# One load moved forward in SP's queue: the residual rows of channel block 2, in a layered convolution and attention kernel

## The chip, the cores and the metric

The kernel runs on one core of one Trainium2 chip. The metric is the device time of one execution in microseconds (us); lower is better. The engines are named as the profile names them: PE (matmuls; PEld are its weight loads), DVE (vector engine), ACT (scalar engine), POOL, and SP, which here only issues transfers to the DMA engines.

## What is computed

Two kinds of layer alternate on an array x of 2048 positions by 512 channels, each added to x after a layer norm:

```python
x = A_u
x = x + _A_ref(_layernorm(x), ...)   # long convolution by FFT over the 2048 positions, one filter per channel
x = x + _B_ref(_layernorm(x), ...)   # local attention: 32 heads of 16, window of 8 at stride 2
x = x + _A_ref(_layernorm(x), ...)
x = x + _B_ref(_layernorm(x), ...)
return x

# inside _A_ref
K = jnp.einsum("dn,dnl,dn->dl", Cc, P, dB).real          # the filters, from the state-space parameters
Yf = Uf * Kf                                             # spectra of u and of K, length 4096
y = irfft2(Yf)[..., :L]; return y + u * Dskip
```

## The kernel before

The work is four stages in a row: `prepare` with `kernel_and_first_conv`, a first `b_layer`, `a_layer`, and a second `b_layer`. The change lies in `kernel_and_first_conv`, which makes the filters K, their spectra, and the first convolution.

The 512 channels are four blocks of 128, dc = 0 to 3. The array X stays in SBUF as 128 partitions of 16 rows of 512 channels, in two halves of 256. For each block the function does this:

- `tables` and `contract` make the filter from products of tables (DVE, then PE in many small matmuls, lines 488 and 491), and `store` and `fetch` turn it by way of DRAM (lines 839 and 846).
- `spectrum` transforms the block of u, and likewise the block of K: a first set of matmuls (line 862), ACT's copy into Z (line 867), a transpose of Z either by DMA (`turn`, line 876) or by PE and ACT (lines 893 and 897), a second set of matmuls (lines 882 to 885), ACT's copy (line 889). `keep` (line 944) stores the spectrum of K in DRAM for the later `a_layer`.
- `residual` (line 928) loads the block's columns of the input once more into X, in place of the normed columns that `spectrum` has read. It must come after the block's first matmuls, and `final` needs it. It is 512 KB in 2,048 pieces of 256 bytes.
- `product` multiplies the two spectra (DVE, lines 952, 957 and 958), `inverse` transforms back (PE lines 972 to 976, copies into VT at line 979), and `final` (lines 996 and 999) adds the residual rows by a matmul with the identity and the result of the last transform, and is copied into X (line 1003).

The last half block of K (half of block 3) has a way of its own, `last(n)` for n = 0 and 1: `spread_rows` (line 1021), copy (1025), first matmuls (1035 and 1037), copy (1040), transpose by PE (1046), copy (1050), second matmuls (1056 and 1057), copy (1061).

What is issued in what order is written out by hand. Every piece of work is an operation of a plan, numbered in the order in which the code names it, and a list of numbers in `ORDERS` gives the order in which they are issued:

```python
order = [int(i) for i in ORDERS[Plan.turn].split()]
for i in order:
    fn, after, way = self.ops[i]
    fn()
```

Each engine takes its own operations in this order, and waits for what each of them needs. Two operations on different engines are ordered only by such a need. The operations that the text speaks of, by engine in their order before the change:

| engine | operations |
|---|---|
| SP | 669 load of the last filter block (line 846); 387 and 577 stores of K's spectra (line 944); 683 transpose of the last spectrum by DMA (line 876); 579 and 580 stores; **355 the reload of block 2** (line 928); 688, 689 and 578 stores |
| PE | 686 second matmuls of the spectrum that 683 turned; 705 first matmuls of `last(0)`; 646 and 656 inverse of block 2 (lines 972, 976); 715 `spread_rows` of `last(1)`; 708 transpose of `last(0)`; 636 inverse of block 2; 718 first matmuls of `last(1)`; 711 second of `last(0)`; 666 `final` of block 2 |
| DVE | 654 join (lines 957, 958) for 656; 633 product and 634 join for 636; 728 and 738 products of block 3 |
| ACT | 682 copy for the store 688; 706 copy of 705's result; 647 copy of 646's; 657 of 656's; 716 of 715's; 709 of 708's |

Op 633 writes into one of two buffers, the one that 646 has read; 728 and 738 wait in the same way for 656 and 636. The pool of accumulators in PSUM has three buffers.

Of the kernel before, what the change touches and what calls it, by code (L numbers as in the profile page):

```python
# [198 lines left out]
def load_params(nc, pp, prm):  # L199
# [33 lines left out]
    "375 431 461 433 533 463 492 494 536 548 526 495 499 498 585 496 539 497 540 500 549 550 553 555 551 556 554 610 "  # L233
    "611 612 613 616 552 586 546 388 449 587 439 617 534 544 572 557 529 618 619 545 614 441 620 622 567 530 451 443 "
    "535 575 562 669 588 589 592 593 598 453 576 560 472 387 561 473 604 469 570 470 670 672 571 671 599 605 673 674 "
    "676 606 675 623 690 691 577 677 692 693 608 679 565 694 624 609 702 680 566 681 682 607 626 627 703 683 579 643 "
    "653 644 696 697 580 698 699 700 654 686 705 355 687 646 706 656 715 647 657 716 708 633 634 709 636 728 738 637 "
    "718 688 711 689 720 666 712 721 722 663 724 578 668 729 739 664 725 727 714 731 748 741 750 732 743 758 759 757 "
    "744 761 762 777 771 768 778 772 774 769 775",
    "82 0 50 136 7 57 84 39 1 93 156 86 128 85 44 154 87 155 40 142 13 241 262 130 58 199 200 201 99 190 263 264 125 "  # L240
# [1791 lines left out]
```

## Time and profile before

| | |
|---|---|
| three runs | 470.94 us median, 469.26 to 471.42 |
| the profiled execution | 470.51 us, of which the span from the first to the last instruction is 468.7 |
| busy in the span | PE 393.3 us (84%), PEld 242.7 (52%), DVE 440.0 (94%), ACT 348.1 (74%), POOL 21.2 (5%) |
| mean granted clock of PE | 0.996 of full speed |
| instructions of PE | 5,229 matmuls and 5,248 weight loads |
| transfers of line 928 | 4, of 512 KB each, 4.9 to 5.8 us from issue to landing, median 5.3 |
| `kernel_and_first_conv` | its last copies into X (line 1003) end at 202 us |

Times inside an execution are counted from the start of the span. A line of a timeline gives the start, the duration, the engine, the source line, the operation, what it writes and reads, and how many were merged (x2). In brackets stands how long the engine was idle before it, and which event the profile holds responsible. A wait for several events is put down to the last of them; where the engine named was done long before, it was something else. "issue" means that nothing in the profile explains the wait. A line of the table by windows gives, for a stretch of time, the busy time of each engine with the number of instructions, the clock granted to PE, the mean busy share of the 16 DMA engines and the GB/s they moved.

### The profile page before, as it was taken

Reading aid. Unit: us, or ns where it says so; the run is one execution under the profiler, and the core shown is the slowest. Engines: PE = TensorE matmul, PEld = TensorE weight load, DVE = VectorE, ACT = ScalarE, POOL = GpSimd, SP = SyncE. Lnnn points to the kernel's source line nnn. Section 1 sums busy time; section 2 is a strip of 40 time slices with the busy share of each in tenths; the row PEclk is TensorE's granted clock in tenths of the full one; section 3 lists DMA queues with packets and bytes.
Section 4 is the critical chain, followed back from the end, with each engine's and each line's share of the span. In section 5 each row is a group of like instructions: output and inputs, shape, how many; then the busy total and the mean of one; then the engine's idle time right before and its main releaser. Section 6 shows DMA issues by size and latency. Waiting matters only on the chain. (4 is left out here: it accounts for less than half of the span.)

```text
span 468.7 us, 12362 instructions
## 1 busy us (share of the span) xinstructions
PE 393.3 (84%) x5229; PEld 242.7 (52%) x5248; DVE 440.0 (94%) x595; ACT 348.1 (74%) x543; POOL 21.2 (5%) x90
## 2 busy tenths in 40 slices
PE   2520876788899997899999979979999999998996
PEld 1310543545666666654476434556776445563453
DVE  6999999999999995879999999999996899999995
ACT  6999867896888886657797357999996667763452
POOL 1000000000000000500000000000000000100210
PEclk9999999999999998999999999999999999999999
DMA  8991163138597564840112230379957200213584
GB/s 233 189 304 71 14 150 91 21 73 162 140 178 148 126 140 134 138 69 1 62 47 78 57 67 2 69 247 183 170 100 111 58 18 18 79 46 78 61 155 123
DMA packets 111419, 49.36 MB, mean 105 GB/s; under 512 B 88811, under 2 KB 104572, under 8 KB 111108
## 3 DMA queue, kind: packets, MB, share of 16 engines
q1 hardware_dynamic: 109924, 47.70, 46.9%
q0 software_dynamic: 1152, 0.61, 1.1%
q8 instruction: 41, 0.67, 0.6%
q10 hardware_dynamic: 288, 0.26, 0.2%
q14 instruction: 14, 0.11, 0.1%
HBM read 15.88 MB, written 8.13 MB: 51 GB/s over the span
## 5 line engine op out<-in xcount | busy, mean ns | idle before, releaser
L1755 DVE TENSOR_TENSOR prod<-VX,L 128x512 bf16<-128x512 bf16 (+2 forms) x72 | 75.2, 1100 | 0.5
L1579 DVE TENSOR_TENSOR prod<-qT,kT 128x4096 bf16<-128x4096 bf16 (+1 forms) x40 | 72.3, 1859 | 1.6 <-ACT qT L1504 1.5
L1771 PE MATMUL po<-prod,sb_ident 128*128 128x512 bf16 x216 | 51.7, 379 | 2.5 <-DVE prod L1755 1.1
L1771 PEld LDWEIGHTS <-sb_ident 128*128 128x128 bf16 x224 | 21.7, 98 | 27.8 <-issue 2.5
L450 PE MATMUL ps_sum<-Ttab,sb_ident 128*128 128x512 bf16 x36 | 14.7, 407 | 22.1 <-DVE Ttab L411 20.6
L1534 PE MATMUL ps_v<-wv,U 128*128 128x256 bf16 x256 | 31.3, 272 | 1.0 <-ACT L L1718 0.3
L867 ACT CAST Z<-ps_s 128x1024 bf16<-128x1024 f32 (+1 forms) x32 | 29.3, 986 | 3.2 <-PE ps_s L862 2.6
L1855 PE MATMUL ps_o<-wo_t,oT 128*128 128x512 bf16 x122 | 31.4, 379 | 0.2
L1545 ACT ACTIVATE VX<-ps_v,rs 128x256 bf16<-128x256 f32 x64 | 26.6, 472 | 4.5 <-PE ps_v L1534 4.1
L1480 PE MATMUL ps_qk<-U,wqk 128*128 128x512 bf16 x128 | 29.7, 379 | 0.2 <-ACT qT L1485 0.2
L1534 PEld LDWEIGHTS <-U 128*128 128x128 bf16 x256 | 24.4, 98 | 8.9 <-issue 4.3
L1499 PE MATMUL ps_qk<-U,wqk 128*128 128x512 bf16 x128 | 29.0, 379 | 0.0
L475 DVE TENSOR_TENSOR Ttab<-Ttab,MPA 128x2048 bf16<-128x2048 bf16 (+2 forms) x20 | 28.3, 1428 | 0.1
L1789 ACT CAST ot<-po 128x1024 bf16<-128x1024 f32 x14 | 13.9, 1013 | 18.0 <-PE po L1771 18.0
L475 DVE TENSOR_TENSOR Y2tab<-Ttab,MPB 128x6144 bf16<-128x6144 bf16 (+1 forms) x13 | 27.2, 2117 | 0.0
L952 DVE TENSOR_TENSOR pa<-sp_u,sp_k 128x2048 bf16<-128x2048 bf16 x16 | 19.3, 1219 | 5.9 <-PE vp L976 4.3
L488 PE MATMUL psk<-Ttab 128*32 128x64 bf16 x1024 | 20.1, 197 | 4.3 <-DVE Ttab L475 3.1
L455 ACT CAST Ttab<-ps_sum 128x1024 bf16<-128x1024 f32 (+1 forms) x22 | 18.1, 869 | 7.0 <-PE ps_sum L451 6.9
L488 PEld LDWEIGHTS <-Ttab 128*32 128x32 bf16 x1024 | 18.0, 95 | 8.8 <-issue 7.4
L412 DVE TENSOR_TENSOR Ttab<-Ttab,MUB 128x256 bf16<-128x256 bf16 (+4 forms) x36 | 22.3, 619 | 0.0
L1590 PE MATMUL Lp<-prod,sb_bones 128*32 128x512 bf16 x256 | 19.7, 382 | 2.6 <-DVE prod L1579 2.4
L491 PE MATMUL psk<-Y2tab,Ttab 128*32 128x48 bf16 x1024 | 19.8, 190 | 1.8 <-DVE Y2tab L475 1.2
(255 smaller groups left out, 1018.0 us busy)
## 6 DMA issues: line engine op xcount, KB each, us to landing
kt_scratch<-sp_k SPq DMA_DIRECT2D x16, 256.0 KB, 4.1
Kt<-kt_scratch SPq DMA_DIRECT2D x16, 256.0 KB, 5.4
X<-in_A_u_dram SPq DMA_DIRECT2D x8, 256.0 KB, 5.4
X<-in_A_u_dram SPq DMA_DIRECT2D x4, 512.0 KB, 5.3
out_dram<-X SPq DMA_DIRECT2D x16, 128.0 KB, 2.3
k_scratch<-KTq SPq DMA_DIRECT2D x7, 256.0 KB, 2.3
KT<-k_scratch SPq DMA_DIRECT2D x7, 256.0 KB, 3.4
VX<-VX SPq DMA_DIRECT2D x4, 448.0 KB, 3.8
```

The costliest lines, as they stand in the source:

```text
L412: nc.vector.tensor_tensor(self.spare(hc, False)[:, x0:x1, :, :, 0:m, :].rearrange("n x h c e t -> n (x h c) e t"), src, mult(1), ALU.mult)
L475: nc.vector.tensor_tensor(d, src.to_broadcast([128, c, n, 2 * EYB]), mm, ALU.mult)
L488: nc.tensor.matmul(o.rearrange("e (s i) -> e s i", s=2), xs, T[:, 1:3, h, m // 2, :, t], start=(m == 0), stop=False, skip_group_check=True)
L867: nc.scalar.copy(box["Z", kind, dc][:, 0:n // 8, :, jq * 32:(jq + 1) * 32].rearrange("p g r k -> p r g k"), box.pop(("s1", kind, dc, jq))[ ...
L1480: nc.tensor.matmul(ps[:], wqk[:, ct, f0:f0 + 128], XT[:, ct // 2, 4 * s:4 * s + 4, ct % 2, :], start=(ct == 0), stop=(ct == 3))
L1499: nc.tensor.matmul(box[name][:, k * 512:k * 512 + 512], wqk[:, ct, f0:f0 + 128], XT[:, ct // 2, 4 * s:4 * s + 4, ct % 2, :], start=(ct == ...
L1534: nc.tensor.matmul(ps[:, jj].rearrange("p t h d -> p (t h d)"), XT[:, ct // 2, j + jj, ct % 2, :], wv[:, ct, fp * 256:(fp + 1) * 256], sta ...
L1545: nc.scalar.activation(out, ps, ACT.Identity, scale=r)
L1579: nc.vector.tensor_tensor(pr[:], windows(q, 0, 2), windows(kT[fp][:, a:a + n2, col(w):col(w) + 1024], -DIL * 128, 2), ALU.mult)
L1755: nc.vector.tensor_tensor(p2[:].rearrange("p w j t d h -> p w (j t) d h"), windows(v, -DIL * 256, taps), l.to_broadcast([128, taps, nj * 2 ...
L1771: nc.tensor.matmul(po[:, c:c + 512], ident[:], p2[:, t, k + j:k + j + 2].rearrange("p j t d h -> p (j t d h)"), start=first, stop=stop)
L1855: nc.tensor.matmul(ps, oT[:, ft // 2, o:o + 128], wo_t[:, ft, :], start=(ft == 0 and not res), stop=(ft == 3))
```

## The change

Op 355, the reload of block 2's residual rows, stands 32 places further ahead in the second list of `ORDERS`: right behind op 577 and ahead of op 677, instead of behind op 705. The order of all other operations stays the same. On SP's queue it passes three operations: 683, 579 and 580. No other function or size is changed.

```diff
-    "676 606 675 623 690 691 577 677 692 693 608 679 565 694 624 609 702 680 566 681 682 607 626 627 703 683 579 643 "
-    "653 644 696 697 580 698 699 700 654 686 705 355 687 646 706 656 715 647 657 716 708 633 634 709 636 728 738 637 "
+    "676 606 675 623 690 691 577 355 677 692 693 608 679 565 694 624 609 702 680 566 681 682 607 626 627 703 683 579 "
+    "643 653 644 696 697 580 698 699 700 654 686 705 687 646 706 656 715 647 657 716 708 633 634 709 636 728 738 637 "
```

## The prediction

> **What bounds the kernel now.** I read the page first. DVE is busy for 94% of the span, PE for 84%. The chain that ended last is followed back only to 421.99 us, far behind the change, so it says nothing here; the stage itself has to be read. The moved reload is the fourth transfer of line 928, and the timeline of SP has it at 174.92:
>
> ```profile
> 164.22 0.57 SPq L846 DMA_DIRECT2D KT<-k_scratch  x1
> 164.85 1.30 SPq L944 DMA_DIRECT2D kt_scratch<-sp_k  x2
> 171.22 2.55 SPq L876 DMA_TRANSPOSE zt<-Z  x1
> 173.83 1.05 SPq L944 DMA_DIRECT2D kt_scratch<-sp_k  x2
> 174.92 0.56 SPq L928 DMA_DIRECT2D X<-in_A_u_dram  x1
> 175.63 4.05 SPq L944 DMA_DIRECT2D kt_scratch<-sp_k  x3
> ```
>
> SP is done with op 577 at 166.15 and then waits until 171.22, when ACT's last copy of the spectrum (line 867) ends. Who reads the reload? Op 666, PE's first matmul of line 996 for block 2, at 188.90. The transfers of line 928 land in 5.3 us at the median, this one by about 180.2: nobody waits for its data, and by that reading alone the move is worth nothing. So I read the stretches around it, with the table by windows (columns: stretch, length, busy time of PE, weight loads, DVE, ACT, POOL, granted clock, DMA share, GB/s):
>
> ```profile
> 168.50:171.80 3.30, 2.76 (x165) 2.48 (x162) 3.30 (x6) 3.03 (x6) 0.00 (x0) 1.00 0.03 9
> 174.50:177.00 2.50, 2.34 (x139) 1.94 (x137) 2.50 (x4) 2.41 (x3) 0.00 (x0) 1.00 0.80 223
> 177.00:179.70 2.70, 2.66 (x45) 1.92 (x44) 2.14 (x5) 2.44 (x4) 0.00 (x0) 1.00 1.05 251
> 179.70:182.30 2.60, 0.00 (x0) 0.00 (x0) 1.99 (x3) 1.09 (x2) 0.00 (x0) 1.00 0.67 234
> 182.30:184.30 2.00, 1.99 (x16) 1.70 (x16) 0.44 (x1) 0.51 (x1) 0.00 (x0) 0.62 0.07 20
> 184.30:186.30 2.00, 2.00 (x21) 1.99 (x20) 0.79 (x1) 1.09 (x2) 0.00 (x0) 0.53 0.00 0
> ```
>
> Until 179 DVE is full (the last table products). Then follows a chain of PE, ACT and DVE steps up to the last copies into X at 202, and in it PE stands still for 2.6 us and then runs at about half clock for 3.4 us, while the DMA engines are full from 174.5 to 181.5 and were empty from 168.5 to 171.8.
>
> Why does PE stand still? The timelines of PE and DVE:
>
> ```profile
> 178.73 0.41 DVE L958 TENSOR_TENSOR pa<-pa 128x512 bf16<-128x512 bf16 x1
> 182.31 0.27 PE L972 MATMUL vp<-sb_IC,pa 128*128 128x256 bf16 x1 [2.64 <-DVE pa L958]
> 111.39 0.39 PE L450 MATMUL ps_sum<-Ttab,sb_ident 128*128 128x512 bf16 x1 [0.88 <-issue]
> 141.12 0.38 PE L884 MATMUL xp<-zt,sb_C 128*128 128x512 bf16 x1 [1.02 <-issue]
> ```
>
> The named releaser ended at 179.14, before PE stopped at 179.66; PE had even loaded op 656's first weights at 179.39. So it was something else. Two other stops (0.88 and 1.02) are inside a group of matmuls that need nothing new, and are put down to "issue". Counting PE's weight loads and matmuls in order of time, the three stops come after instructions 3,262, 4,542 and 6,334: the differences, 1,280 and 1,792, are 5 and 7 times 256. And the DMA part of the page has a queue that carries instructions:
>
> ```profile
> q8 instruction: 41, 0.67, 0.6%
> ```
>
> 41 packets of 16 KB for PE's 10,477 instructions are 256 instructions each. Narrowing the DMA view to single packets gives their times: 108.34 to 110.08, 138.78 to 139.70, 179.93 to 180.97. PE resumes 1.31, 1.42 and 1.34 us after each of them ends. PE stands still because its next block of instructions is not there. The 24th block was due to be asked for when PE entered the block before, at 175.9; its packet starts 4.0 us later. The two blocks ahead of it started 0.2 us before and 1.0 us after that point (166.53, 171.83). What lies in those 4.0 us is the reload: 2,048 pieces of 256 bytes, which run from 176.5 to 179.8. The block's packet comes just behind them.
>
> **The change, part by part.** Nothing is added or removed. SP issues op 355 straight after op 577, past three operations of its own queue: the transpose 683 and the stores 579 and 580. No other engine's order changes, POOL's queue has nothing here.
>
> *The issue itself.* One issue of 0.56 us goes from 174.92 to about 166.2. It lies in SP's wait up to 171.22 (5.1 us), so it costs nothing; without that cover it would delay the transpose by 0.56. The matmuls of block 2's forward transform, which it must follow, ended before 149 (the later reload of block 3 is issued then), so it adds no wait. Behind it on SP stand 683, 579, 580; 683 feeds PE's op 686 at 176.74.
>
> *The transfer.* In front of it are the load of line 846 and two stores, whose packets end at 168.5. The reload's pieces took about 3 us, so here they run from 168 to 171 through the empty stretch and land by about 171.5 to 172. The transpose's packets begin at 172.2. Nothing collides; from below nothing is gained, from above the transpose waits out the whole 3 us: it landed 4.0 us after its issue, at 175.2, 1.5 before its reader, so at most 1.5 us are lost on PE. I take nothing, the nearer row being the DMA share of 0.03.
>
> *What leaves 176.5 to 179.8.* Ahead of the 24th block remain the stores 579 and 580 (packets over at about 176.7) and 688, which waits for ACT until 175.60 and stays at 175.63. With the start of the two blocks before (0.2 before to 1.0 after the point), a length of 1.04 to 1.57 and 1.3 to 1.4 to arrive, it is there between 178.0 and 179.9; PE needs it at 179.5. If it waits for all of 688 too (8 packets of 84 ns on each engine, 0.7), 180.6. The stop shrinks from 2.64 to between 0 and 1.1; I take 0.2.
>
> *The clock.* It fell at 182.78 for 3.41 us, after the 2.64 us stop and not after those of 0.88 and 1.02. At 0.62 and 0.53 of full clock, 4.0 us of PE work held 0.76 + 0.94 = 1.7 us of loss. Below nothing is impossible here; at the other end a shorter stop still drops the clock. I take 1.7 as regained.
>
> *What is late next.* Without the stop, op 656 runs from 179.5 to 180.6, 715 to 181.5, 708 to 182.0. Op 636 then waits for DVE's join 634, which ends at 181.78 before and after, since its own start (179.76) waits for op 646, ahead of the stop. So 636 starts at 181.9 instead of 186.10: 4.2 us. ACT keeps up (657 to 181.8, 716 to 182.3, 709 to 183.3, in time for 711 at 183.8 instead of 188.04), and DVE's op 728 comes at 181.8 instead of 183.86, 738 at 183.0 instead of 187.28. From there each step waits for the one before, as now, up to X at 202, and all later stages start from X. **Sum:** 2.64 + 1.7 = 4.3, held to 4.2 by join 634, less 0.2 of stop left: 4.0. The profiled execution took 470.51 (span 468.7 and 1.8 around it): 466.5. The median, 470.94, is 0.4 above it, which gives 466.9. I say **466.7**.
>
> **The rivals.**
> 1. *A shorter gain.* The block still waits for 688, or the clock still falls: stop 1.1 (gain 3.1), or stop 0.5 with the clock loss (gain 2.0). 467.4 to 468.9. For it: block 17 began only as two stores drained (138.78).
> 2. *The reload is not what holds the block.* Then only 0.56 us of SP time moves and the time stays at 470.5 to 470.9. For it: the stores of line 944 crowd the same stretch. Against: blocks 22 and 23, the first of them beside two such stores, started within 1.0.
> [...] The trace has the block wait 4.0 us, until the reload's pieces are through.
> [...]
> 3. *Slower: the 23rd block is late instead.* It started at 171.83, 0.4 ahead of the transpose's pieces. If the reload's tail holds it beyond 172.2, it falls behind them too (to 174.3), as block 12 did at 105.8 to 108.3. It then arrives at 174.3 + 1.5 + 1.3 = 177.1, while PE needs it from 175.9: 1.2 us lost. If the stores and 688 still hold block 24 for 4 us, its stop is moved, not removed, and a second fall of the clock adds 1.7: 470.5 + 1.2 + 1.7 = 473.4. It decides from a tail beyond 172.2. Against: the pieces should be through at 171.
>
> **How the numbers follow.** Forecast 0.62, rival 1 0.13, rival 2 0.17, rival 3 0.08. The lowest run is 1.7 under the median; taken off the 466.7 that is 465.0, the low end; the high end, 470.9, takes in rivals 1 and 2 up to the median. A measurement here tells about 0.5%, 2.4 us, from no change. Faster by more (below 468.6): forecast and half and more of rival 1, 0.70. Within: 0.22. Slower: 0.08.
>
> **What would show it.** The reload at 166.2 on SP; DMA share high at 168.5 to 171.8 and lower at 177 to 179.7; the 24th packet of q8 before 177.5; no stop of PE over 0.5 us before op 656; the clock at 1.00 through 182 to 186; op 636 near 182. Wrong if q8's packet stays near 180, if a stop appears at 175.9, or if X is ready 4 us earlier and the end is not.

## The result and the profile after

| kernel | median of 20 runs | lowest to highest |
|---|---|---|
| before | 470.09 us | 468.8 to 472.57 |
| after | 468.51 us | 467.26 to 471.95 |

The ratio is 0.9958, with a 95% interval of 0.994 to 0.9976. A second comparison of the same two kernels (y_after below) gave 0.9965 (0.9945 to 0.9985). The change wins about 1.6 to 2 us; 4.0 were forecast. The profiled execution of after took 469.76 us, 1.25 above its median, so the two profiles must be compared stretch by stretch and not by their ends.

The timeline of SP after the change (start, duration, line, operation):

```profile
166.63 1.15 SPq L944 DMA_DIRECT2D kt_scratch<-sp_k  x2
167.82 0.57 SPq L928 DMA_DIRECT2D X<-in_A_u_dram  x1
172.88 2.27 SPq L876 DMA_TRANSPOSE zt<-Z  x1
175.19 5.87 SPq L944 DMA_DIRECT2D kt_scratch<-sp_k  x5
```

The reload goes out right behind the two stores, inside SP's wait, and the transpose is not held up: it starts 1.66 us later than before, but everything at this place runs 1.4 us later in this execution, from stops of PE at 69.7 us and between 111 and 144, ahead of anything that was moved, and it lands 3.6 us after its issue (4.0 in before). The stores' packets run to 171.9 and the reload's pieces from 170.0 to 173.7; the transpose's own begin at 174.1. The same stretches in the table by windows:

```profile
168.50:171.80 3.30, 2.93 (x50) 1.88 (x51) 3.30 (x7) 2.99 (x6) 0.00 (x0) 1.00 0.96 271
174.50:177.00 2.50, 2.50 (x27) 1.75 (x24) 2.50 (x6) 1.81 (x3) 0.00 (x0) 1.00 0.98 176
177.00:179.70 2.70, 2.70 (x153) 2.06 (x153) 2.70 (x4) 2.56 (x5) 0.00 (x0) 1.00 0.58 201
179.70:182.30 2.60, 2.11 (x35) 1.79 (x32) 1.99 (x4) 2.47 (x3) 0.00 (x0) 1.00 0.47 169
182.30:184.30 2.00, 2.00 (x32) 1.93 (x31) 1.97 (x4) 1.66 (x3) 0.00 (x0) 1.00 0.17 50
184.30:186.30 2.00, 2.00 (x41) 1.48 (x40) 1.42 (x3) 1.67 (x2) 1.24 (x1) 1.00 0.02 4
```

The DMA share (last column but one) rose from 0.03 to 0.96 where the engines had been empty, and fell from 1.05 to 0.58 at 177 to 179.7. PE, which did nothing from 179.7 to 182.3, is busy for 2.11 us there, and the granted clock (the column ahead of the DMA share) stays at 1.00 where it was 0.62 and 0.53.

The timeline of PE, with op 656 first, and two idle times of later stages that will matter:

```profile
181.57 0.27 PE L972 MATMUL vp<-sb_IC,pa 128*128 128x256 bf16 x1 [0.49 <-ACT Zu L1040]
...
270.72 0.61 PE L1696 MATMUL ps_den<-L,sb_ident 128*128 128x128 bf16 x8 [2.06 <-ACT L L1705]
...
311.17 2.08 PE L1182 MATMUL ps_s<-U,sb_F 128*128 128x128 bf16 x25 [1.92 <-ACT Z L1186]
```

The stop of 2.64 us is 0.49 now. The packet of block 24 starts 1.94 us after PE entered the block before it (4.1 in before). The 0.49 has two possible ends, which this trace can't tell apart: ACT's copy of line 1040 ends at 181.29, and the packet ended 1.40 us before PE resumed.

**Where the time went.** The same DVE instructions, one by one, after minus before: 0 up to 71.8 us, +0.9 at 73, +1.4 from 144 to 181, then -2.4 from op 738 (187.3) on. So the stage won 3.8 us, as forecast. Two losses lie outside it. Ahead of it, 1.4 us: PE stopped for 1.54 at 69.68, at another boundary of instruction blocks, which in before's profile passed without a stop. Behind it, 1.6 us: the clock fell at 271.7 and 312.6, right behind the two idle times shown above:

```profile
268.30:271.70 3.40, 1.20 (x14) 0.72 (x16) 3.40 (x3) 2.24 (x4) 0.00 (x0) 0.99 0.24 46
271.70:275.10 3.40, 3.40 (x33) 1.38 (x26) 3.30 (x3) 1.23 (x4) 0.00 (x0) 0.50 0.56 106
309.20:312.60 3.40, 1.41 (x23) 1.23 (x22) 3.40 (x6) 3.40 (x5) 0.00 (x0) 1.00 1.04 389
312.60:316.00 3.40, 3.40 (x35) 3.30 (x33) 1.53 (x3) 2.85 (x5) 0.00 (x0) 0.50 0.52 122
```

Before has the same two idle times (2.06 at 271.04, 1.92 at 310.89) and no fall behind either. Two questions follow: is it really the reload that holds block 24, and what does the median win, if one execution's stage wins 3.8?

### The profile page after: what moved, and what is told of

The parts are those of the page before. It is cut to its first block, busy times and chain, and to the rows that moved or that the text cites. A ratio compares the mean times of both kernels' runs of the same rounds, so it can differ in the third digit from the quotient of the medians.

```text
span 468.0 us, 12380 instructions
## 1 busy us (share of the span) xinstructions
PE 396.0 (85%) x5248; PEld 243.6 (52%) x5248; DVE 440.1 (94%) x595; ACT 347.7 (74%) x543; POOL 21.2 (5%) x90
## 5 line engine op out<-in xcount | busy, mean ns | idle before, releaser
L1590 PE MATMUL Lp<-prod,sb_bones 128*32 128x512 bf16 x256 | 21.0, 411 | 1.9 <-DVE prod L1579 1.7
```

## The experiments

Theory A is the forecast's: the pieces of the reload hold block 24. B: the stores of line 944 crowd it. C: chance between executions. D: something else that the early reload brings (rows there earlier, SP's queue shorter).

**x_none: no reload of block 2 at all.** It leaves out that load, so the rows of block 2 are added to what `final` finds in X.

```diff
-            Rd[dc] = pl.op("S", 0.7, residual, *fs, lag=5.2)
+            Rd[dc] = pl.op("S", 0.7, residual if dc != 2 else lambda: None, *fs, lag=5.2)
```

> The kernel before with block 2's residual reload left out (its rows in X stay the normed ones, so the residual of that block is not the reference's). Theory A, the reload's pieces hold up PE's 24th block of instructions: as fast as the changed kernel, 0.994 to 0.998 of before; the packet of q8 that carries the block starts within 1.5 us of PE's entering the block ahead of it; PE stops 0 to 0.7 us ahead of op 656, and the clock does not fall there. Rival B, the stores of line 944 crowd out the block and the reload only lies among them: the stop stays at 2 to 2.6 us, the time at 0.999 to 1.001. Rival C, the difference is chance (other stops of PE and falls of the clock): any of both, and the stop ahead of op 656 does not go with the time.

Measured: 0.9958 (0.9931 to 0.9984), the same as the change. In its profile block 24's packet starts 1.56 us after PE entered the block before; no stop; the stage is 4.1 us shorter than in before. The table by windows, at the place of the stop:

```profile
177.00:179.70 2.70, 2.70 (x152) 2.06 (x148) 2.70 (x5) 2.37 (x4) 0.00 (x0) 1.00 0.39 135
179.70:182.30 2.60, 2.56 (x42) 2.21 (x39) 1.88 (x4) 2.56 (x4) 0.00 (x0) 1.00 0.49 175
```

All five stores of line 944 are still there, so B falls for this place; no rows come early, so that half of D falls with it. SP's queue is shorter here too, by the one issue, so x_none alone doesn't exclude the other half. Before's rows do: there the reload's issue ended at 175.48, and the store behind it, op 688, waited for ACT until 175.60 in any case.

**x_late: the reload behind op 689 instead of ahead of 677.**

```diff
-    ... 686 705 355 687 646 706 ... 718 688 711 689 720 666 ...
+    ... 686 705 687 646 706 ... 718 688 711 689 355 720 666 ...
```

> The kernel before with op 355 moved the other way, to behind op 689: its issue falls at about 179.2 instead of 174.9, its pieces at 180 to 183. Theory A: block 24, asked for at 175.9, is no longer held up, so the stop ahead of op 656 shrinks to 0 to 0.7 us although the reload is later; it lands at 184 to 185, when op 666 (184.6 without the stop) reads it, at most 0.7 us lost: 0.994 to 0.999 of before. Rival D, what helps is that the rows are in place earlier, or that SP's queue is free earlier: the same as before or slower, 1.000 to 1.005. Rival B: the stop stays, 0.999 to 1.002.

Measured: 0.9965 (0.9943 to 0.9986). The timelines of SP and PE, with the first matmul of block 24, which has no wait that the view notes:

```profile
181.98 0.57 SPq L928 DMA_DIRECT2D X<-in_A_u_dram  x1
182.57 0.27 PE L972 MATMUL vp<-sb_IC,pa 128*128 128x256 bf16 x1
```

The reload goes out at 181.98; block 24's packet starts 1.02 us after its point; no stop. Op 666 waits 0.39 us for the rows. Earlier or later does the same: what matters is that the reload isn't there between 176 and 180, in before's times.

**x_twice: the change, and the same reload once more behind op 580.**

```diff
+                if (dc, c) == (2, 3):
+                    nc.sync.dma_start(columns(X, slice(0, NJ), 2), xv[:, :, 2 * DCH:3 * DCH])
```

> The changed kernel with the same reload issued a second time at its old place, right behind op 580 (it writes the same rows again). Theory A: the pieces lie once more where block 24 is asked for; the stop of 1.5 to 2.7 us is back, the time is that of before, 0.998 to 1.001. Rivals C and D: the early reload keeps its gain, 0.994 to 0.998, with no stop ahead of op 656; a second load that op 666 waits for costs nothing, since it lands near 180 as it does before.

Measured: 1.0003 (0.9984 to 1.0022); the gain is gone. The timeline of PE and the windows (the matmul of op 656 has line 975 in this file):

```profile
182.76 0.27 PE L975 MATMUL vp<-sb_IC,pa 128*128 128x256 bf16 x1 [1.65 <-DVE pa L955]
```

```profile
182.30:184.30 2.00, 1.53 (x20) 1.44 (x20) 1.29 (x4) 0.47 (x1) 0.00 (x0) 1.00 0.41 150
184.30:186.30 2.00, 2.00 (x35) 1.78 (x32) 1.03 (x2) 2.00 (x4) 0.04 (x1) 1.00 0.00 0
```

The second reload goes out at 175.74, block 24's packet starts 3.41 us after its point, and the stop is back at the same instruction. But it is 1.65 long and not 2.64, and the clock did not fall behind it. That was the first sign that the size of the stop is not fixed.

**x_shift: before, with 128 more PE instructions at about 20 us** (the row sums of line 677 formed twice).

```diff
-                for ct in range(4):
+                for ct in range(8):
-                    nc.tensor.matmul(..., xT[:, ct // 2, j, ct % 2, :], ..., start=(ct == 0), stop=(ct == 3), ...)
+                    nc.tensor.matmul(..., xT[:, ct % 4 // 2, j, ct % 2, :], ..., start=(ct % 4 == 0), stop=(ct % 4 == 3), ...)
```

> The kernel before, its reload where it was, with 128 instructions more for PE at about 20 us (the row sums of line 677 are formed twice, where PE has time), so that every boundary between blocks of 256 instructions comes 128 instructions earlier in the work. Theory A: no boundary lies ahead of op 656 any more, so the stop of 2.6 us there goes; the next boundary comes 128 instructions later, in op 718, and its block, asked for at about 176.4, is held by the reload until 182, when PE is about to need it: a stop of 0 to 0.7 us there. Every other boundary moves too, so the whole time is uncertain: 0.992 to 1.000. Rivals B, C and D, in which the stop ahead of op 656 has another cause (a join, a store, a slot in PSUM): it stays at 2 to 2.6 us, since no order, no transfer and no need is changed.

Measured: 1.0251 (1.022 to 1.0281). The time misses the expectation widely. Of the place of the stop the trace says what theory A says: op 656 starts without a stop, and count 6,334 now falls into the middle of `contract`, where PE stands still:

```profile
190.61 0.19 PE L491 MATMUL psk<-Y2tab,Ttab 128*32 128x48 bf16 x1
192.90 0.20 PE L491 MATMUL psk<-Y2tab,Ttab 128*32 128x48 bf16 x3 [2.10 <-issue]
```

Stops of 1.85 to 3.00 us appear at five other counts that are 190 to 194 modulo 256 (1,727, 2,754, 3,774, 4,542 and 5,310; before's page has 5,229 matmuls and after's 5,248 for the same work, so counts differ by a few), for the other boundaries moved too, into stretches where PE runs through a block quickly (in before's profile 128 matmuls of `contract` and as many weight loads start within 1.02 us). The six stops come to 13.2 us; the kernel is 12 us slower. What held block 24 this run doesn't show: its packet begins at 190.17, more than 2.6 us after PE entered the block before, just as the packets of two stores of line 944 end (190.16) and 0.7 us into the reload's pieces (189.5 to 193.6).

**How large is the stop in other executions?** Four kernels went into the next comparison, two of them unchanged copies.

y_before (before once more): 

> The kernel before, unchanged, for a second profile. Theory A (the reload's pieces hold block 24, in every execution): a stop of PE at count 6,334 again, 1.5 to 3 us, and block 24's packet 3 us or more after PE entered the block before. The forecast's second part (the clock falls because of this stop) holds if the clock falls within 2 us of the stop's end here too; if it falls elsewhere, the 1.7 us belonged to one execution and the change can win them only in some. Theory C (chance): no stop above 0.8 us at 6,334. Ratio 1.000.

y_after (the change once more): 

> The changed kernel, unchanged, for a second profile and more times. Theory A: no stop at count 6,334 above 0.6 us, block 24's packet within 2.5 us of the request; 0.9958 of before, as in the first comparison. The clock may fall anywhere behind a longer idle time of PE; if in this profile it falls at fewer places than in the first (271.7 and 312.6 us there), the time is nearer to 467, which would show that chance falls of the clock hide part of the gain. Theory C: 1.000.

y_first:

```diff
-    "142 139 129 143 93 94 140 64 96 ... 28 153 131 166 222 ..."
+    "142 139 129 143 93 94 140 96 ... 28 153 131 166 64 222 ..."
```

> Only block 0's reload is moved, from 62.95 us (SP, line 928, the first of four) to behind the load of line 846 that ended about 73.9; nobody reads its rows before 134. Theory A: it is block 6 of the instructions that it holds, and PE's stop at count 1,727 to 1,729 (1.17 and 1.54 us in the two profiles) goes or falls under 0.5: 0.7 to 1.2 us less, 0.9975 to 0.9985 of before. The stop at 6,334 stays. Rival: the stop there comes from the two transposes and the load of line 846 beside it and stays; 1.000. Other rival: moved behind 73.9 it holds block 8 or the transposes at 74.4, and the time rises by 1 us.

y_all (the change, y_first's move, and op 164 from ahead of 343 to behind 322):

> The change, and with it block 0's reload as in the run before, and block 1's reload from 116.45 us to behind the store of line 839 that ended at 96.7, where SP then waits until 105.8; read first at 164. Theory A: the stop at 6,334 gone (2 us), that at 1,729 gone (0.7 to 1.2), that at 3,518 (0.55 and 1.35 us) smaller: 2.5 to 3.5 us in all, 0.9925 to 0.995 of before, 0.7 to 1.5 us below the change alone. Rival (DVE is full until 179, and takes up what PE wins earlier): no better than the change, 0.9958.

Measured: y_before 1.0011 (0.9986 to 1.0036), y_after 0.9965 (0.9945 to 0.9985), y_first 0.9993 (0.9969 to 1.0017), y_all 0.9955 (0.993 to 0.9981). In y_first and y_all no stop is left at count 1,727, but y_before and y_after have none there either: that stop comes in some executions only (the 1.17 that the expectation gives for before is a wait for ACT's line 867, at another count). So the earlier moves bring nothing that these runs can tell.

**z_before, z_after, z_all: the two late idle times filled,** in before, in the change, and in y_all.

```diff
                     ps = box["den", fp, j0] = psA.tile([128, 128], F32, name="ps_den", tag="psA")
+                    for w in range(12):
+                        nc.tensor.matmul(ps[:], ident[:], ident[:], start=True, stop=True)
...
-                for jj in range(nj):
+                box["n"] = box.get("n", 0) + 1
+                for jj in list(range(nj)) * (3 if box["n"] == 4 else 1):
```

> The kernel before, with PE kept busy in its two long idle times of the later stages: 12 matmuls of the identity with itself ahead of each sum of line 1696 (into the same accumulator, written over by the sum), and the fourth group of line 1182 formed three times. The idle times of 2.06 us (271.04) and 1.92 us (310.89) then stand at some 1.2 and 0.9. Theory L (a fall of the clock comes where an idle time of 1.8 us or more lies in one stretch of 3.41 us, and the two late ones cost 0.5 and 0.9 us in about half of the executions, in both kernels): no fall between 260 and 320, the one behind the stop at 6,334 stays; 0.3 to 1.0 us below before, 0.998 to 0.9995. Rival: the late falls have another cause and stay, or the added instructions (some 170) bring new stops; 1.000 or above.

> The changed kernel with the same two additions. Theory L: no fall of the clock between 60 us and the last stretch of the span; 0.5 to 1.2 us below the change alone: 466.8 to 467.8 median where the change alone has 467.9 to 468.5, 0.9925 to 0.995 of before; the gap to the run before, with the late falls out of both, is the stop and such falls as it brings: 2.5 to 3.5 us. If the gap stays at 2 us, it is not the late falls that took back part of the local 4 us, but that in many executions of before the stop brings no fall. Rival as in the run before: no gain from the additions.

> The change, the reloads of blocks 0 and 1 moved too, and the same two additions: the candidate for the best. Theory L and the moves: 0.9915 to 0.9945 of before. If the earlier moves bring nothing, as their runs without the additions had it (0.9955 against 0.9965 for the change alone, within the uncertainty), it equals the run before.

Measured: z_before 1.0013 (0.9988 to 1.0038), z_after 0.9977 (0.996 to 0.9993), z_all 0.9981 (0.9961 to 1.0001). The falls did go, as the windows of z_after show (granted clock 1.00; 0.50 in the second half of both places in after):

```profile
268.00:275.00 7.00, 5.15 (x61) 2.71 (x61) 6.89 (x5) 4.76 (x7) 0.00 (x0) 1.00 0.41 79
307.00:315.00 8.00, 6.75 (x97) 5.48 (x94) 6.77 (x12) 8.00 (x11) 0.00 (x0) 1.00 0.78 219
```

But the additions cost what they win: instruction by instruction against before, DVE of z_before loses 0.8 us between 245 and 258 and 1.1 between 324 and 337. No version beat the change by more than the runs can tell, and theory L (the late falls took back part of the 4 us) falls as an explanation of the small gain: with the late falls out of both kernels, the means of 12 runs are 471.01 and 469.04, still only 1.97 apart. What the runs show instead is in how they spread. z_after lies between 468.1 and 470.32. z_before has two groups: nine runs at 469.76 to 470.88 (mean 470.32) and three at 472.62, 472.94 and 473.75 (mean 473.10). The three have a mean granted clock of 0.991 to 0.996 (one fall, 3.41 us at 0.50 in a span of 468.7, takes 0.0036), seven of the nine 0.999 or more; of the other two one has 0.996, and one, the profiled one, 0.96 from a low clock at 15 to 53 us, far ahead of the stage. Against z_after's mean the nine are 1.28 slower, the three 4.07. And z_before's profiled execution is one of the nine:

```profile
177.70 0.39 PE L882 MATMUL xp<-zt,sb_C 128*128 128x512 bf16 x1
181.45 0.27 PE L972 MATMUL vp<-sb_IC,pa 128*128 128x256 bf16 x1 [0.82 <-ACT Zu L1040]
```

```profile
177.00:179.70 2.70, 2.65 (x70) 1.90 (x68) 2.14 (x5) 1.51 (x2) 0.00 (x0) 1.00 1.07 259
179.70:182.30 2.60, 1.78 (x18) 1.45 (x15) 1.54 (x2) 2.02 (x3) 0.00 (x0) 1.00 0.59 208
182.30:184.30 2.00, 2.00 (x32) 1.93 (x31) 1.58 (x3) 1.78 (x3) 0.00 (x0) 1.00 0.04 9
```

The old order, with the DMA engines as full as before (1.07), and yet a stop of 0.82 and no fall. In this execution the transpose ahead of the reload held SP for 1.97 us and not 2.55, the reload went out at 174.33 and not 174.92, and block 24's packet started at 178.62, not 179.93.

The 0.82 is not the whole loss. PE also came to the boundary 0.97 us later: op 686 (line 882) starts at 177.70, in before at 176.74. The last 128 matmuls of `contract` ahead of it took 1.99 us, in before 1.02. The reload's pieces began in the middle of them (176.13), but that alone doesn't explain it: in after 128 matmuls of `contract` ran beside the reload's pieces (171.8 to 172.8) in 1.03. What slowed them is open.

All profiles but x_shift's together (delay: from PE's entry into the block before to the start of block 24's packet; a dash is a stop under 0.25 us; stage: how much less time than in before's profile passes on DVE from 175 us to op 738; falls in the last 6 us of the span are left out):

| profile | reload among the stores | delay, us | stop | clock falls behind it | other falls after 60 us | stage, us | time |
|---|---|---|---|---|---|---|---|
| before | yes | 4.10 | 2.64 | yes | none | 0 | 470.51 |
| y_first | yes | 3.63 | 2.39 | yes | 313.3 | 0.3 | 471.44 |
| y_before | yes | 3.14 | 2.06 | yes | 312.8 | 0.6 | 470.89 |
| x_twice | yes | 3.41 | 1.65 | no | 312.2 | 2.3 | 470.60 |
| z_before | yes | 2.80 | 0.82 | no | none | 2.5 | 470.61 |
| after | no | 1.94 | 0.49 | no | 271.7, 312.6 | 3.8 | 469.76 |
| z_after | no | 1.70 | 0.28 | no | none | 4.0 | 468.49 |
| y_all | no | 1.65 | - | no | 269.1, 310.0 | 4.2 | 467.73 |
| x_none | no | 1.56 | - | no | 270.6, 311.5 | 4.1 | 468.67 |
| z_all | no | 1.55 | - | no | none | 4.3 | 468.16 |
| y_after | no | 1.18 | - | no | 310.3 | 4.4 | 467.87 |
| x_late | no | 1.02 | - | no | 171.1, 273.5 | 2.0 | 470.36 |

x_late's stage holds 2.1 us that it lost by 180 us, behind its fall at 171.1 and ahead of the boundary. Less that, the stage is 3.8 to 4.4 us shorter than before's wherever the reload is out of the way. Where it is in the way, the stage is 0 to 0.6 us shorter with a fall behind the stop, and 2.3 to 2.5 without one: so in these two the reload costs only some 1.3 to 2.1 us.

## Why the prediction was right, and which term was too large

*The mechanism.* Right. The reload holds block 24 (x_none, x_late: stop gone; x_twice: stop back), and the stop is that of a block (x_shift: it goes with the count). Rival 2, that the reload isn't what holds the block, is refuted: block 24's packet waited 2.8 to 4.1 us in all five profiles with the reload in front of it, and 1.0 to 1.9 in the seven without. In the five it began 2.4 to 3.3 us after the reload's first piece, and from 0.5 us before the last one to just behind it. In before's profile the pieces run from 176.68 to 179.92, and the packet starts at 179.93. When a block is asked for was the author's reading, since no trace shows a request: what is measured is the start of a packet against PE's entry into the block before, and the other 40 packets of q8 in before's profile start between 3.8 us ahead of that entry and 1.9 us behind it (block 24's 4.0 behind).

*The issue and the transfer.* Right in effect: at 167.82 the issue lies in SP's wait, and the transpose is not late. But the pieces took 3.7 us, not 3, and met the stores' packets; their end at 173.7 is 172.3 in before's times, where the prediction has 171 and rival 3 begins to count from 172.2. Rival 3 (block 23 late) still did not come: its packet starts 1.01 us after its point, and PE has no stop there.

*The stop that is left.* 0.2 forecast, 0.49 in the first profile, 0.28 in z_after, under 0.25 in y_after.

*What is late next.* Op 636 was forecast at 181.9, in before's time. It starts at 183.78, less the 1.4 us that this execution runs late 182.4. From there the lead stays constant up to 275.9, so nothing between gives it back.

*The size.* This is where it failed: "The profiled execution took 470.51 [...]: 466.5. The median, 470.94, is 0.4 above it, which gives 466.9." The sum, 2.64 of stop and 1.7 of clock, was right for that one execution, and was taken off the median as if every execution lost it. The stop of 2.64 is the longest of the five that were seen; the others are 0.82 to 2.39. The clock fell behind three of them. The 12 runs of z_before put it in figures: 4.07 us in three of them, 1.28 in nine, 1.97 in the mean. The forecast describes the first kind and the median is of the second. That the three longer runs are those with a fall behind the stop is inferred from their mean clock; they have no trace of their own. Runs without any addition point the same way: beside y_after, before's seven runs with a mean clock of 1.000 have a mean of 468.33, the change's two 467.22, only 1.11 apart. The median that the sum started from was of three runs as well; over 20 runs it is 470.09, 0.85 lower. Rival 1 (a shorter gain, 467.4 to 468.9) gave the right time, by luck: neither of the two reasons that it named was the cause. The measured 468.51 lies in the stated range because that took in the rivals' times, not because the sum was right for the median.

*What stays open.* Why before's profile, with both losses, is not above its median: part of the answer is that it had no stop at 69.7 and no late fall, which other executions have, but the shares of these were not counted. How often the stop brings a fall is open too: three of the five profiles have one, and three of z_before's twelve runs by their mean clock. And why PE came to the boundary 0.97 us later in z_before's profile is not known.

## What to carry to other kernels

Where an engine stops for one or two microseconds inside a group of instructions that needs nothing new, count its instructions: if the stops are multiples of one number apart (here 256: 41 packets of q8 for 10,477 instructions of PE, and stops 1,280 and 1,792 apart), look for the packet of its next block and for what the DMA engines do between the engine's entry into the block before and that packet. A transfer that fills them there, like this one of 2,048 pieces (DMA share 1.05 at 177 to 179.7), is worth trying where they are empty (0.03 at 168.5 to 171.8). The stop here had no fixed length: 0.82 to 2.64 us in five profiles, with a fall of the clock behind three of them. Before a stop and its clock loss are put into a sum, take a second profile, or forecast the median from the shorter of the cases.

## What the runs showed of the hardware

*The clock falls on a grid.* Within an execution, the starts of the falls after 50 us are whole multiples of 3.413 us apart (before: 286.72, 84 times; after: 40.96, 12 times; y_before: 129.7, 38 times), and each fall that the end of the span doesn't cut lasts 3.41 us. The grid lies differently in each execution: in steps of 3.413 us from the start of the span, the falls come 1.9 us behind a step in before, 0.9 in x_none and 0.4 in x_late. The clock fell behind idle times of PE that are shorter than one step: 2.64 us in before's profile, 2.06 and 1.92 in after's. With the edges of the grid taken from each execution's own falls, 19 idle times of PE between 50 us and the last 6 us of the span lie with 1.8 us or more between two edges (ten profiles, without the z runs), and the clock fell behind 18 of them; of the shorter ones, two were followed by a fall (1.37 and 1.55 between two edges, with shorter ones beside them). So whether an idle time of 2 us cost a fall went, with one exception (1.88 in y_after), by where an edge happened to lie: in before's profile the 2.06 us at 271.04 was cut into 0.49 and 1.57, the 1.92 at 310.89 into 1.60 and 0.32, and nothing fell; in after's both lay whole between two edges (268.25 to 271.67, 309.21 to 312.62), and the clock fell at 271.67 and 312.62.

*A block of instructions is late by more than its transfer.* Block 24's packet takes 0.9 to 1.5 us (1.04 in before, 1.00 in after), and where PE stood waiting for it, it went on 1.3 to 1.6 us after the packet's end (1.34 in before). In before's profile PE came to the first instruction of block 24 some 3.8 us after it entered the block before (175.83 to 179.66); less 1.04 for the packet and 1.34 behind it, 1.4 us were left for the packet to begin. In the profiles with the reload in front it took 2.8 to 4.1. What such crossings can cost x_shift shows: with 128 more instructions PE stops for 1.85 us or more at six of them, 13.2 us in all.
